# q in 512-byte packets, a state product on column tiles, a second issuing queue and a new order of the first loads in a fused retention and channel-mix kernel

## Chip, cores, metric

The kernel runs on one core of one Trainium2 chip. The metric is device time in microseconds (us) of one execution; lower is better. Some executions fall into a slower state of the chip, about 1.7% longer. Only fast executions are compared, and ratios are of executions on the same chip in the same rounds.

## The reference

Two layers follow each other. The first is a linear attention with a decay per head (4 batches, 8 heads, 768 tokens, 64 elements a head); the second is a channel mix with weights of 512x1024, 1024x512 and 512x512.

```python
for t in range(S):                       # retention, per batch b and head h
    state = gamma[h] * state + outer(k[t], v[t])
    y[t] = (q[t] @ state) / sqrt(D)
x = y.transpose(0, 2, 1, 3).reshape(B, S, H * D)
x_prev = shift x by one token
xk = mu_k * x + (1 - mu_k) * x_prev      # and xr with mu_r
k = maximum(xk @ w_k, 0)
out = sigmoid(xr @ w_r) * (k * k @ w_v)
```

## The kernel before

Tokens go in 24 chunks of 128 (six a batch). Each chunk is loaded as k, q, v with eight heads side by side, cast to 16 bits, and transposed on TensorE, so that the elements of two heads lie on 128 partitions. Then four products follow, named here by the letters used throughout: A (k with q, two heads at a time on two row tiles of the array), Y (v with the masked A, on two column tiles), I (the state of the last chunk with q, on the full array, since the state is kept block-diagonal for two heads) and S (the new state). The channel mix has Z (with w_k), R (with w_r) and V (with w_v). A list scheduler inside the kernel decides, from estimated durations, in which order each engine's instructions are emitted, and puts "filler" matmuls, whose results nobody reads, where it expects TensorE to be idle in the first 60 us. Constants at the top steer it.

```python
BLOCKS = {0: ((1,), (1,), (1, 1), (1, 1)), 3: ((1, 1), (1, 1), (1,), (1,))}
STORE = 5.0
FIRST = "k0 c2 q0 c16 c32 v0 k1 q1 v1 mu wk0 k2 q2 v2 wk1 wr k3 q3 v3 wv0 k4 q4 v4 wv1".split()
# ...
    def filler(b):
        nc.tensor.matmul(b.tile[:, 0:256], lhsT=warm[:, 0:P], rhs=warm, start=True, stop=True)
# ... every load: 128 tokens on partitions, 8 heads of 64 floats: 256 B runs
            src = s[b, :, c * C : (c + 1) * C, :].rearrange("h t d -> t h d")
            ... nc.sync.dma_start(out=t32.tile[:, n], in_=src)
# ... A: row tiles r = partitions 0:64 and 64:128
                nc.tensor.matmul(
                    pA.tile[:, hp, j], lhsT=t[r, 1, j, :], rhs=t[r, 0, j, :], ...)
# ... I: full array, four matmuls
                for j in range(NJ):
                    nc.tensor.matmul(
                        y()[:, j, :], lhsT=s_prev.tile[:, j], rhs=qkT.tile[:, 0, j, :],
                        start=(j == 0), stop=False, skip_group_check=True)
# ... Y: column tiles, eight matmuls into the same accumulator
            for j, hp, r in heads:
                nc.tensor.matmul(
                    y()[r, j, :], lhsT=v16.tile[:, 2 * j + hp, :], rhs=a2t.tile[:, hp, j, :], ...)
```

Of the kernel before, what the change touches and what calls it, by code (L numbers as in the profile page):

```python
# [21 lines left out]
BLOCKS = {0: ((1,), (1,), (1, 1), (1, 1)), 3: ((1, 1), (1, 1), (1,), (1,))}  # L22
BLOCKS_ELSE = ((2,), (2,), (2,))
STORE = 5.0
FIRST = "k0 c2 q0 c16 c32 v0 k1 q1 v1 mu wk0 k2 q2 v2 wk1 wr k3 q3 v3 wv0 k4 q4 v4 wv1".split()
BUFS = dict(t32=5, qks=3, v16=5, qkT=3, a2t=3, xT=2, dx=1, xk=2, xr=1, krel=3, k2=8, rsb=4,
            osb=5, w32=4)
COST = dict(qk=0, qkT=4000, relu=300, mask=0, dx=4000, s=500, v=0, w=800)
# [30 lines left out]
class Plan:  # L59
# [21 lines left out]
    def order(self):  # L81
        taken = {tag: [] for tag in self.bufs}
        free = {e: 0.0 for e in self.LAT}
        free["DMA"] = 1100.0
# [120 lines left out]
def kernel(  # L205
# [12 lines left out]
    nc = tc.nc  # L218
# [13 lines left out]

    gam = 1.0 - 2.0 ** (-5.0 - np.arange(H, dtype=np.float64))
    ar = np.arange(C, dtype=np.float64)
    h_pj = 2 * np.arange(NJ)[None, :] + (np.arange(P) // 64)[:, None]
# [10 lines left out]
    dec = [0.125 * gam[None, :] ** (ar + (par - 1) * C)[:, None] for par in range(2)]  # L246
# [3 lines left out]
    causal_np = (ar[None, :] >= ar[:, None]).astype(np.float64)  # L250
# [74 lines left out]

    def dma(dur, out_, in_):
        return Way("DMA", dur, lambda: nc.sync.dma_start(out=out_, in_=in_))  # L327
# [17 lines left out]
    nc.scalar.preload_act_table(AF.Sigmoid)  # L345
# [4 lines left out]
    k_c16 = add(first("c16"), dma(200, c16, c16d.ap()))  # L350
    d0 = add(first("mu"), dma(50, murow[0:4], moe_mu_k.rearrange("(co ci) -> co ci", ci=P)))
# [16 lines left out]
    def weight(dkey, key, w16, wd):  # L368
# [3 lines left out]
        def wide():  # L372
# [4 lines left out]
            dve(1230, lambda: nc.vector.tensor_copy(out=w16, in_=wide()), port=True),  # L377
# [5 lines left out]
    for i in range(2):  # L383
        fs = slice(i * dff // 2, (i + 1) * dff // 2)
        k_wk.append(weight(first(f"wk{i}"), -1.0, wk16[:, :, fs], wkd[:, :, fs]))
# [5 lines left out]
    heads = [(j, hp, slice(hp * 64, hp * 64 + 64)) for j in range(NJ) for hp in range(2)]  # L391

# [3 lines left out]
    def load(bt, b, c):  # L396
# [4 lines left out]
        for i, s in enumerate((k, q, v)):  # L401
            n = (1, 0, 2)[i]
            src = s[b, :, c * C : (c + 1) * C, :].rearrange("h t d -> t h d")
            bt.ld[c].append(add(
                first("kqv"[i] + str(g), g - LA[2] - 0.6 + 0.01 * i), Way("DMA", 1350, lambda n=n, src=src: nc.sync.dma_start(  # L405
                    out=t32.tile[:, n], in_=src)),
                after=[Order(x) for x in bt.ld[c][-1:]],
                takes=[] if i else [t32], uses=[t32] if i else []))

    def attention(bt, b, c):  # L410
# [5 lines left out]
        pT, pA, a2t, pY = Buf("px"), Buf("pA"), Buf("a2t"), Buf("px")  # L416
        e_qks = add(key, [
            dve(690, lambda: nc.vector.tensor_copy(out=qks.tile, in_=t32.tile[:, 0:2]), port=True),
            act(1010, lambda: nc.scalar.copy(out=qks.tile, in_=t32.tile[:, 0:2]),  # L419
# [12 lines left out]
        def do_T():  # L432
            o = pT.tile.bitcast(F16).rearrange("p (a j c) -> p a j c", a=2, j=NJ)
            for j in range(NJ):
                for i in range(2):
# [13 lines left out]

        def do_A():  # L450
            t = qkT.tile
            for j, hp, r in heads:
                nc.tensor.matmul(  # L453
                    pA.tile[:, hp, j], lhsT=t[r, 1, j, :], rhs=t[r, 0, j, :],
# [4 lines left out]
        def mask(i, takes, uses, after):  # L459
# [7 lines left out]
                out=a2t.tile[:, i], in_=a2t.tile[:, i], pattern=[[0, NJ], [1, C]],  # L467
# [7 lines left out]
        if c + 1 < NCH:  # L475
# [5 lines left out]
            def do_S():  # L481
                for j in range(NJ):
                    nc.tensor.matmul(  # L483
                        pS.tile[:, j], lhsT=qks.tile[:, 1, 2 * j : 2 * j + 2, :],
                        rhs=v16.tile[:, 2 * j : 2 * j + 2, :],
# [29 lines left out]
        if c > 0:  # L515
            def do_I():
                for j in range(NJ):
                    nc.tensor.matmul(  # L518
                        y()[:, j, :], lhsT=s_prev.tile[:, j], rhs=qkT.tile[:, 0, j, :],
                        start=(j == 0), stop=False, skip_group_check=True)  # L520

            e_I = add(key + 0.3, pe(220, do_I), after=[e_qkT, e_sprev], takes=[pY],
                      uses=[qkT, s_prev], mode="full")

        def do_Y():
            for j, hp, r in heads:
# [176 lines left out]
```

## Time and profile before

| | before |
|---|---|
| time, median of the runs beside the kernel after | 177.98 us (177.04 to 179.74) |
| span of the profiled execution | 176.0 us |
| TensorE busy | 170.0 us (97%) |
| VectorE busy | 142.6 us (81%) |
| first V, in effect | 38.8 us |
| end of the last V | 172.1 us |

"First V in effect" is the start of the fifth V matmul, the first that needs the second half of w_v, minus four matmuls of 0.2155 us. The end of the last V is the start of its last matmul plus 0.2155. The first V in effect is the mark at which the start, bound by transfers, hands over to the stretch bound by TensorE. The views that show these two regimes are in the prediction below. From the first V in effect to the end of the last is 133.3 us; the emitted matmuls and changes of mode make 132.2 of it.

### The profile page before, as it was taken

How to read it: one execution, taken by the hardware profiler on the slowest of the kernel's cores; microseconds unless marked ns; L12 is line 12 of the kernel's file. 1: busy time of each engine (PE TensorE's matmuls, PEld its weight loads, DVE VectorE, ACT ScalarE, POOL GpSimd, SP SyncE). 2: the span in 40 equal slices, each digit the busy share in tenths (PEclk: the TensorE clock that was granted, in tenths of full speed). 3: DMA queues.
4: the chain of work that ended last, by engine and by line, in shares of the span. 5: the costliest groups of instructions: out<-in, count | busy, mean ns of one | idle time of the engine just before them, and what ended most of it. 6: DMA issues, size and time to landing. Idle time of an engine off the chain costs nothing.

```text
span 176.0 us, 4319 instructions
## 1 busy us (share of the span) xinstructions
PE 170.0 (97%) x1777; PEld 116.5 (66%) x1777; DVE 142.6 (81%) x248; ACT 114.8 (65%) x161; POOL 45.9 (26%) x55
## 2 busy tenths in 40 slices
PE   7999999999999999999999999999999999899991
PEld 5587977866956766756758658648477567494850
DVE  0377797969879989999989899999998945897731
ACT  2432266554997876978965958969759575755550
POOL 3041010111433425237351263333214103400000
PEclk9999999999999999999999999999999999999999
DMA  4999999799989989899999967927330013010202
GB/s 105 231 300 268 378 199 308 178 298 192 234 171 249 253 202 264 208 240 233 228 260 227 261 117 187 255 46 186 112 119 4 0 63 119 2 62 24 96 29 94
DMA packets 81304, 30.79 MB, mean 175 GB/s; under 512 B 75514, under 2 KB 75650, under 8 KB 81284
## 3 DMA queue, kind: packets, MB, share of 16 engines
q1 hardware_dynamic: 81284, 30.51, 72.6%
q8 instruction: 14, 0.23, 0.6%
q14 instruction: 6, 0.05, 0.1%
HBM read 24.22 MB, written 6.29 MB: 173 GB/s over the span
## 4 chain that ended last, share of the span: by engine, by line
PE 72%; SPq 14%; DVE 5%; DMA 4%; ACT 2%; issue 1%; DVEq 0%; ACTq 0%
PE pm L639 24%; PE pm L603 21%; SPq L405 11%; PE pm L632 10%; PE px L436 5%; DMA t<-in_q_dram 4%; PE pA L453 3%; PE px L527 3%; PE px L518 2%; PE pS L483 2%; SPq L375 2%; SPq L327 2%; PE pm L277 1%; DVE xr L572 1%; PE pS L492 1%
## 5 line engine op out<-in xcount | busy, mean ns | idle before, releaser
L466 POOL TENSOR_SCALAR_AFFINE_SELECT a2t<-a2t 128x512 f16<-128x512 f16 x31 | 23.9, 783 | 89.7 <-ACT a2t L464 87.7
L603 PE MATMUL pm<-xk,wk 128*128 128x128 f16 (+1 forms) x576 | 47.0, 237 | 0.0
L639 PE MATMUL pm<-wv,k 128*128 128x512 f16 x192 | 44.9, 379 | 0.5 <-ACT k L622 0.5
L603 PEld LDWEIGHTS <-wk 128*128 128x128 f16 x576 | 40.1, 98 | 4.5 <-DVE wk L377 0.4
L446 ACT COPY qkT<-px 128x1024 f16<-128x1024 f16 x24 | 24.2, 1012 | 16.8 <-PE px L436 16.6
L639 PEld LDWEIGHTS <-k 128*128 128x128 f16 x192 | 18.0, 98 | 20.9 <-ACT k L622 0.7
L616 ACT ACTIVATE krel<-pm 128x512 f32<-128x512 f32 x34 | 20.3, 600 | 15.1 <-PE pm L603 14.8
L572 DVE SCALAR_TENSOR_TENSOR xk<-dx,mu,xT 128x256 f16<-128x256 f32 (+1 forms) x56 | 27.9, 537 | 0.1
L572 DVE SCALAR_TENSOR_TENSOR xr<-dx,mu,xT 128x256 f16<-128x256 f32 (+1 forms) x56 | 25.9, 498 | 1.0 <-PE pm L632 0.9
L622 ACT ACTIVATE k<-krel 128x1024 f16<-128x1024 f32 x24 | 25.4, 1060 | 0.3
L424 POOL TENSOR_TENSOR v<-t,c_sb 128x512 f16<-128x512 f32 x17 | 20.7, 1219 | 17.1 <-DMA t<-in_v_dram 13.0
L277 PE MATMUL pm<-warm 128*128 128x256 f16 x164 | 23.6, 290 | 1.1 <-DVE xT L536 1.1
L650 DVE SCALAR_TENSOR_TENSOR osb<-pm,rsb 128x512 f32<-128x512 f32 x24 | 16.4, 684 | 10.2 <-PE pm L639 5.0
L632 PE MATMUL pm<-wr,xr 128*128 128x512 f16 x96 | 24.2, 380 | 0.0
L464 ACT CAST a2t<-pA 128x512 f16<-128x512 f32 x31 | 17.4, 588 | 9.4 <-PE pA L453 7.2
L277 PEld LDWEIGHTS <-warm 128*128 128x128 f16 x164 | 15.8, 103 | 5.5 <-DVE xT L536 1.1
L419 ACT CAST qks<-t 128x1024 f16<-128x1024 f32 x16 | 16.7, 1052 | 2.4 <-DMA t<-in_q_dram 2.4
L542 DVE TENSOR_TENSOR xT<-px,Gy 128x512 f32<-128x512 f32 x24 | 16.3, 681 | 0.8 <-PE px L527 0.8
L645 ACT ACTIVATE rsb<-pm 128x512 f32<-128x512 f32 x24 | 14.0, 602 | 4.0 <-PE pm L632 3.9
L462 DVE TENSOR_TENSOR a2t<-pA,c_sb 128x512 f16<-128x512 f32 x17 | 11.6, 688 | 5.1 <-ACT a2t L464 4.7
L563 DVE TENSOR_TENSOR dx<-xT 128x1024 f32<-128x1024 f32 (+1 forms) x14 | 15.3, 1090 | 0.3
L436 PE MATMUL px<-c_sb,qks 128*128 128x128 f16 x192 | 14.5, 219 | 0.1
(34 smaller groups left out, 131.2 us busy)
## 6 DMA issues: line engine op xcount, KB each, us to landing
t<-in_k_dram SPq DMA_DIRECT2D x24, 256.0 KB, 4.6
t<-in_q_dram SPq DMA_DIRECT2D x24, 256.0 KB, 5.2
t<-in_v_dram SPq DMA_DIRECT2D x24, 256.0 KB, 5.3
out_dram<-osb SPq DMA_DIRECT2D x24, 256.0 KB, 3.8
w<-in_moe_w_k_dram SPq DMA_DIRECT2D x2, 1024.0 KB, 6.5
w<-in_moe_w_v_dram SPq DMA_DIRECT2D x2, 1024.0 KB, 7.4
w<-in_moe_w_r_dram SPq DMA_DIRECT2D x1, 1024.0 KB, 9.4
c_sb<-c SPq DMA_DIRECT2D x1, 64.0 KB, 3.7
```

Source lines behind the costliest of these rows:

```text
L277: nc.tensor.matmul(b.tile[:, 0:256], lhsT=warm[:, 0:P], rhs=warm, start=True, stop=True)
L405: first("kqv"[i] + str(g), g - LA[2] - 0.6 + 0.01 * i), Way("DMA", 1350, lambda n=n, src=src: nc.sync.dma_start(out=t32.tile[:, n], in_=src)),
L424: return lambda: engine.tensor_tensor(out=v16.tile, in0=t32.tile[:, 2], in1=Gv[par].unsqueeze(2).broadcast_to([P, H, D]), op=ALU.mult)
L436: nc.tensor.transpose(o[:, i, j, :], qks.tile[:, i, 2 * j : 2 * j + 2, :], ident)
L446: act(1010, lambda: nc.scalar.copy(out=qkT_out(), in_=pT.tile.bitcast(F16))),
L466: f = add(key + 0.2, pool(700, lambda: nc.gpsimd.affine_select(out=a2t.tile[:, i], in_=a2t.tile[:, i], pattern=[[0, NJ], [1, C]], compare_ ...
L572: (200 + TM) / 0.96, lambda w=w, o=o, co=co: nc.vector.scalar_tensor_tensor(out=cut(o)[:, co], in0=cut(dx)[:, co], scalar=mu[:, w * NCO + ...
L603: nc.tensor.matmul(o[:, n], lhsT=wk16[:, co, fo * P : fo * P + P], rhs=cut(xk)[:, co, t0 : t0 + TM], start=(co == 0), stop=(co == NCO - 1))
L616: act(600, lambda pZ=pZ, o=r_out: nc.scalar.activation(out=o(), in_=pZ.tile, func=AF.Relu, scale=KSC)),
L622: e_sq.append(add(kz + 0.05, act(1060, lambda krel=krel, k2=k2: nc.scalar.activation(out=k2.tile, in_=krel.tile, func=AF.Square)), after=e ...
L632: nc.tensor.matmul(pR.tile, lhsT=cut(xr)[:, co, t0 + ts.start : t0 + ts.stop], rhs=wr16[:, co, :], start=(co == 0), stop=(co == NCO - 1))
L639: nc.tensor.matmul(pV.tile, lhsT=o[:, n, ts], rhs=wv16[:, fo, :], start=(fo == 0), stop=(fo == NFO - 1))
```

## The change

The intent has four parts. q is loaded two tokens at a time, so that a packet has 512 B instead of 256; each q load becomes two, one for even and one for odd heads, each into every second row. This permutes q's tokens within a chunk (columns with a stride of two) and the heads that share a column block. I then is run head by head on column tiles, eight matmuls of half the width. The constants of the scheduler were searched anew; chunk 4 now follows all weights. And the first q load and the constants are issued from ScalarE's queue, ahead of the load of ScalarE's function table.

```diff
-FIRST = "k0 c2 q0 c16 c32 v0 k1 q1 v1 mu wk0 k2 q2 v2 wk1 wr k3 q3 v3 wv0 k4 q4 v4 wv1".split()
+FIRST = "k0 q0 c2 c16 c32 mu v0 k1 q1 v1 k2 q2 v2 wk0 wk1 k3 q3 v3 wr wv0 wv1".split()
+BY_ACT = ("q0", "c2", "c16", "c32", "mu")
 # BLOCKS, STORE, BUFS, COST: other values (cut)
+            def q_load(src=src, name=name):
+                for i in range(2):
+                    queue(name).dma_start(
+                        out=t32.tile[i::2, 0].rearrange("p (h s) d -> p h (s d)", s=2),
+                        in_=src.rearrange("(h i) (p s) d -> i p h (s d)", i=2, s=2)[i])
 # cast of q and k: rearranged heads (cut); A:
-                    pA.tile[:, hp, j], lhsT=t[r, 1, j, :], rhs=t[r, 0, j, :],
+                    pA.tile[:, hp, j], lhsT=t[r, 1, j, :], rhs=q_cols(j, r),   # [..., i::2]
 # I:
-                for j in range(NJ):
+                for j, hp, i, yj in cols2:
                     nc.tensor.matmul(
-                        y()[:, j, :], lhsT=s_prev.tile[:, j], rhs=qkT.tile[:, 0, j, :],
+                        y()[i * 64 : i * 64 + 64, yj, :], lhsT=s_prev.tile[:, j, hp],
+                        rhs=q_cols(j, slice(0, P)), ...)
-            e_I = add(key + 0.3, pe(220, do_I), ..., mode="full")
+            e_I = add(key + 0.3, pe(240, do_I), ..., mode="col")
 # the square of relu may also go to GpSimd; x is written with a stride of two (cut)
```

More of the change, by code (lines that the diff above doesn't have):

```diff
@@ L21 @@
 LA = (2.0, 0.4, 3.5)
-BLOCKS = {0: ((1,), (1,), (1, 1), (1, 1)), 3: ((1, 1), (1, 1), (1,), (1,))}
+BLOCKS = {0: ((1,), (1,), (1,), (1,), (1, 1)), 3: ((2,), (2,), (1, 1))}
 BLOCKS_ELSE = ((2,), (2,), (2,))
-STORE = 5.0
-FIRST = "k0 c2 q0 c16 c32 v0 k1 q1 v1 mu wk0 k2 q2 v2 wk1 wr k3 q3 v3 wv0 k4 q4 v4 wv1".split()
-BUFS = dict(t32=5, qks=3, v16=5, qkT=3, a2t=3, xT=2, dx=1, xk=2, xr=1, krel=3, k2=8, rsb=4,
+STORE = 4.0
+FIRST = "k0 q0 c2 c16 c32 mu v0 k1 q1 v1 k2 q2 v2 wk0 wk1 k3 q3 v3 wr wv0 wv1".split()
+BY_ACT = ("q0", "c2", "c16", "c32", "mu")
+BUFS = dict(t32=5, qks=3, v16=5, qkT=2, a2t=2, xT=2, dx=1, xk=3, xr=1, krel=2, k2=6, rsb=4,
             osb=5, w32=4)
-COST = dict(qk=0, qkT=4000, relu=300, mask=0, dx=4000, s=500, v=0, w=800)
+COST = dict(qk=0, qkT=1200, relu=300, mask=0, dx=4000, s=500, v=100, w=2000, wd=100, sq=200)
 class Buf:
@@ L83, in order @@
         free = {e: 0.0 for e in self.LAT}
-        free["DMA"] = 1100.0
+        free["DMA"], free["ACT"] = 1100.0, 4800.0
         left = {e: [] for e in self.LAT}
@@ L229, with head @@
     INV_KSC2 = 1.0 / (KSC * KSC)
+    def head(j, hp):
+        return 4 * (j // 2) + 2 * hp + j % 2
     gam = 1.0 - 2.0 ** (-5.0 - np.arange(H, dtype=np.float64))
     ar = np.arange(C, dtype=np.float64)
-    h_pj = 2 * np.arange(NJ)[None, :] + (np.arange(P) // 64)[:, None]
+    h_pj = np.array([[head(j, p // 64) for j in range(NJ)] for p in range(P)])
     own = (np.arange(P)[:, None] // 64 == np.arange(2)[None, :]).astype(np.float64)
@@ L244 @@
     c32_np = np.concatenate(cols, axis=1).astype(np.float32)
-    dec = [0.125 * gam[None, :] ** (ar + (par - 1) * C)[:, None] for par in range(2)]
+    tq = 2 * (np.arange(C) % 64) + np.arange(C) // 64
+    dec = [0.125 * gam[None, :] ** (tq + (par - 1) * C)[:, None] for par in range(2)]
     c2_np = np.concatenate(
@@ L249 @@
         axis=1).astype(np.float32)
-    causal_np = (ar[None, :] >= ar[:, None]).astype(np.float64)
+    causal_np = (tq[None, :] >= ar[:, None]).astype(np.float64)
     c16_np = np.concatenate([np.eye(P), causal_np], axis=1).astype(np.float16)
@@ L324, in pe, with queue @@
         return Way("PE", dur, emit)
+    def queue(name):
+        return nc.scalar if name in BY_ACT else nc.sync
     def dma(dur, out_, in_):
-        return Way("DMA", dur, lambda: nc.sync.dma_start(out=out_, in_=in_))
+        return Way("DMA", dur, lambda: nc.scalar.dma_start(out=out_, in_=in_))
     class Order:
@@ L344 @@
     nc.vector.memset(warm, 0.0)
-    nc.scalar.preload_act_table(AF.Sigmoid)
+    add(-97.0, act(0, lambda: nc.scalar.preload_act_table(AF.Sigmoid)))
     wkd = moe_w_k.rearrange("(co ci) f -> ci co f", ci=P)
@@ L376, in weight @@
         return add(key, [
-            dve(1230, lambda: nc.vector.tensor_copy(out=w16, in_=wide()), port=True),
+            dve(1230, lambda: nc.vector.tensor_copy(out=w16, in_=wide()), port=True, cost=COST["wd"]),
             act(1900, lambda: nc.scalar.copy(out=w16, in_=wide())),
@@ L384 @@
         fs = slice(i * dff // 2, (i + 1) * dff // 2)
-        k_wk.append(weight(first(f"wk{i}"), -1.0, wk16[:, :, fs], wkd[:, :, fs]))
+        k_wk.append(weight(first(f"wk{i}"), -1.0, wk16[:, :, fs], wkd[..., fs]))
     k_wr = weight(first("wr"), -0.9, wr16, wrd)
@@ L391 @@
     heads = [(j, hp, slice(hp * 64, hp * 64 + 64)) for j in range(NJ) for hp in range(2)]
+    cols2 = [(2 * a + i, hp, i, 2 * a + hp) for a in range(2) for hp in range(2) for i in range(2)]
     class Batch:
@@ L401, in load, with kv_load @@
         for i, s in enumerate((k, q, v)):
-            n = (1, 0, 2)[i]
-            src = s[b, :, c * C : (c + 1) * C, :].rearrange("h t d -> t h d")
+            src = s[b, :, c * C : (c + 1) * C, :]
+            name = "kqv"[i] + str(g)
+            def q_load(src=src, name=name):
[3 more added lines that the diff above has]
+                        in_=src.rearrange("(h i) (p s) d -> i p h (s d)", i=2, s=2)[i])
+            def kv_load(n=(1, 0, 2)[i], src=src):
+                nc.sync.dma_start(out=t32.tile[:, n], in_=src.rearrange("h t d -> t h d"))
             bt.ld[c].append(add(
-                first("kqv"[i] + str(g), g - LA[2] - 0.6 + 0.01 * i), Way("DMA", 1350, lambda n=n, src=src: nc.sync.dma_start(
-                    out=t32.tile[:, n], in_=src)),
+                first(name, g - LA[2] - 0.6 + 0.01 * i),
+                Way("DMA", (1350, 890, 1350)[i], (kv_load, q_load, kv_load)[i]),
                 after=[Order(x) for x in bt.ld[c][-1:]],
@@ L416, in attention, with cast_args @@
         pT, pA, a2t, pY = Buf("px"), Buf("pA"), Buf("a2t"), Buf("px")
+        def cast_args():
+            return dict(
+                out=qks.tile.rearrange("p n (a i h) d -> p (n a) i h d", a=2, i=2),
+                in_=t32.tile[:, 0:2].rearrange("p n (a h i) d -> p (n a) i h d", a=2, i=2))
         e_qks = add(key, [
-            dve(690, lambda: nc.vector.tensor_copy(out=qks.tile, in_=t32.tile[:, 0:2]), port=True),
-            act(1010, lambda: nc.scalar.copy(out=qks.tile, in_=t32.tile[:, 0:2]),
+            dve(690, lambda: nc.vector.tensor_copy(**cast_args()), port=True),
+            act(1010, lambda: nc.scalar.copy(**cast_args()),
                 cost=COST["qk"])],
@@ L448, in attention, with q_cols @@
             after=[e_T], takes=[qkT], uses=[pT])
+        def q_cols(j, r):
+            a, i = j // 2, j % 2
+            return qkT.tile[r, 0, 2 * a : 2 * a + 2, i::2]
         def do_A():
@@ L466, in mask @@
             f = add(key + 0.2, pool(700, lambda: nc.gpsimd.affine_select(
-                out=a2t.tile[:, i], in_=a2t.tile[:, i], pattern=[[0, NJ], [1, C]],
+                out=a2t.tile[:, i], in_=a2t.tile[:, i], pattern=[[0, NJ], [1, 2], [2, 64]],
                 compare_op=ALU.is_ge, fill=fill0, base=0, channel_multiplier=-1)),
@@ L484, in do_S @@
                         pS.tile[:, j], lhsT=qks.tile[:, 1, 2 * j : 2 * j + 2, :],
-                        rhs=v16.tile[:, 2 * j : 2 * j + 2, :],
+                        rhs=v16.tile[:, head(j, 0) : head(j, 0) + 3 : 2, :],
                         start=(j == 0 and par == 0), stop=(j == NJ - 1), skip_group_check=True)
@@ L516, in do_I @@
             def do_I():
-                for j in range(NJ):
+                for j, hp, i, yj in cols2:
                     nc.tensor.matmul(
-                        y()[:, j, :], lhsT=s_prev.tile[:, j], rhs=qkT.tile[:, 0, j, :],
-                        start=(j == 0), stop=False, skip_group_check=True)
-            e_I = add(key + 0.3, pe(220, do_I), after=[e_qkT, e_sprev], takes=[pY],
-                      uses=[qkT, s_prev], mode="full")
+                        y()[i * 64 : i * 64 + 64, yj, :], lhsT=s_prev.tile[:, j, hp],
+                        rhs=q_cols(j, slice(0, P)), start=(yj == 0), stop=False,
+                        skip_group_check=True)
+            e_I = add(key + 0.3, pe(240, do_I), after=[e_qkT, e_sprev], takes=[pY],
+                      uses=[qkT, s_prev], mode="col")
         def do_Y():
-            for j, hp, r in heads:
+            for j, hp, i, yj in cols2:
                 nc.tensor.matmul(
-                    y()[r, j, :], lhsT=v16.tile[:, 2 * j + hp, :], rhs=a2t.tile[:, hp, j, :],
-                    start=(j == 0 and c == 0), stop=(j == NJ - 1), skip_group_check=True)
-        e_Y = add(key + 0.3, pe(225, do_Y), after=[e_m0, e_m1, e_I],
+                    y()[i * 64 : i * 64 + 64, yj, :], lhsT=v16.tile[:, head(j, hp), :],
+                    rhs=a2t.tile[:, hp, j, :], start=(yj == 0 and c == 0), stop=(yj == NJ - 1),
+                    skip_group_check=True)
+        e_Y = add(key + 0.3, pe(240, do_Y), after=[e_m0, e_m1, e_I],
                   takes=[pY] if c == 0 else [], uses=[v16, a2t] + ([pY] if c else []), mode="col")
@@ L539, in x_out, with y_in @@
         def x_out():
-            return bt.x.tile[:, :, 1 + c * C : 1 + (c + 1) * C]
+            return bt.x.tile[:, :, 1 + c * C : 1 + (c + 1) * C].rearrange(
+                "p j (m i) -> p j i m", i=2)
+        def y_in(t):
+            return t.rearrange("p j (i m) -> p j i m", i=2)
         bt.e_x.append(add(key + 0.3, dve(690, lambda: nc.vector.tensor_tensor(
-            out=x_out(), in0=y(), in1=Gy[:, par], op=ALU.mult)),
+            out=x_out(), in0=y_in(y()), in1=y_in(Gy[:, par]), op=ALU.mult)),
             after=[e_Y, z, k_gy[par]], uses=[bt.x, pY]))
@@ L621, in moe_block @@
             if i % 2:
-                e_sq.append(add(kz + 0.05, act(1060, lambda krel=krel, k2=k2: nc.scalar.activation(
-                    out=k2.tile, in_=krel.tile, func=AF.Square)), after=e_r, takes=[k2],
-                    uses=[krel]))
+                e_sq.append(add(kz + 0.05, [
+                    act(1060, lambda krel=krel, k2=k2: nc.scalar.activation(
+                        out=k2.tile, in_=krel.tile, func=AF.Square)),
+                    pool(1900, lambda krel=krel, k2=k2: nc.gpsimd.tensor_tensor(
+                        out=k2.tile, in0=krel.tile, in1=krel.tile, op=ALU.mult), cost=COST["sq"])],
+                    after=e_r, takes=[k2], uses=[krel]))
         k2s = sorted({id(x[0]): x[0] for x in where.values()}.values(), key=id)
```

## The prediction

> **What bounds the kernel now.** I read the page first, then a table by stretches (busy time of each engine, then of the filler matmuls alone), then the chain of waits, then the timeline where the chain turns from a wait on a transfer to TensorE.
>
> ```profile
> PE   7999999999999999999999999999999999899991
> DVE  0377797969879989999989899999998945897731
> DMA  4999999799989989899999967927330013010202
> GB/s 105 231 300 268 378 199 308 178 298 192 234 171 249 253 202 264 208 240 233 228 260 227 261 117 187 255 46 186 112 119 4 0 63 119 2 62 24 96 29 94
> DMA packets 81304, 30.79 MB, mean 175 GB/s; under 512 B 75514, under 2 KB 75650, under 8 KB 81284
> ```
>
> TensorE looks full from the second slice, and so do the DMA engines until about 104 us. Nearly all packets are under 512 B: they are the 256 B rows (64 floats of a head) of q, k and v. A slice is 4.4 us. In the first 44 us the slices with little but such loads move 178 to 199 GB/s, the best slice, with weight loads (2 KB rows), 378.
>
> TensorE's fullness in the start is made of fillers. In the next two fences the columns are the stretch, its length, busy time and count of each engine, the clock, the DMA share and GB/s; the first has TensorE, weight loads, VectorE, ScalarE and GpSimd, the second TensorE and weight loads of the filler line alone.
>
> ```profile
> 0.00:34.00 34.00, 32.45 (x344) 24.84 (x344) 21.98 (x41) 14.95 (x20) 5.72 (x12) 1.00 0.98 245
> 77.00:104.00 27.00, 27.00 (x261) 17.30 (x256) 25.53 (x41) 22.24 (x32) 12.36 (x14) 1.00 1.09 237
> 104.00:140.00 36.00, 36.00 (x355) 23.78 (x354) 34.51 (x57) 27.50 (x39) 11.26 (x13) 1.00 0.45 111
> ```
>
> ```profile
> 0.00:34.00 34.00, 20.92 (x146) 14.14 (x146) 1.00 0.98 245
> 34.00:45.00 11.00, 2.69 (x21) 1.63 (x18) 1.00 1.02 248
> 45.00:172.00 127.00, 0.00 (x0) 0.00 (x0) 1.00 0.66 153
> ```
>
> So there are two regimes: a start bound by transfers, which ends where the last weight arrives, and a long stretch bound by TensorE, with VectorE 95% busy beside it (25.53 of 27, 34.51 of 36). The chain (start, length, what) and the timeline show the border:
>
> ```profile
> 26.31 7.12 DMA t<-in_q_dram
> 33.53 0.70 DVE qks L418
> 34.27 0.62 PE px L436 x8
> ...
> 37.40 0.33 PE pA L453 x8
> 37.73 1.09 PE pm L277 x9
> 38.82 3.56 PE pm L639 x16
> 42.39 0.45 PE px L436 x8
> ...
> 172.35 0.69 DVE osb L650
> ```
>
> ```profile
> 38.36 1.23 DVE L377 CAST wv<-w 128x2048 f16<-128x2048 f32 x1 [1.49 <-DMA w<-in_moe_w_v_dram]
> ```
>
> The second half of w_v lands at 38.3 us and is cast; the first product with w_v (L639, "V") begins at 38.8. From there to 172.3 is 133.5 us. How much of it is real work? Take issue times from the chain: V and the w_r product 0.2155 us a matmul, the w_k product 0.056 (128 columns) or 0.1105 (256), transposes 0.0556, the row- and column-tiled A and Y 0.028 each (pairs run together), state products 0.055. A group of eight A takes 0.33 instead of 0.224 and the V after it 1.83 instead of 1.73: each change between full, row-tiled and column-tiled array costs about 0.108 us. Over the emitted order, work after the first V is 124.7 us, and 69 changes cost 7.5: 132.2 of 133.5. TensorE hardly stalls there. The chain's detour through ScalarE and VectorE at 68 to 77 us is no stall either: the matmuls in it sum to the same 8.3 us.
>
> **What the Trainium skill says.** (1) "DMA: Bandwidth & Descriptors", Specifications, gives 512 B as the smallest transfer for line rate. The trace agrees in direction: about 185 GB/s with 256 B rows against up to 378 with 2 KB rows; it has no 512 B rows. (2) The same page, "Issuing engines are not separate DMA queues": a second issuing engine saves only issue time. The trace of before has one queue, so doesn't show it. (3) "TensorE: Matmul & The Clock Gate", Part 3, says that column tiles run concurrently. Agreed: eight Y matmuls fit in 0.34 us with one change of mode. (4) "SBUF — State Buffer", Door 1, on 16-byte lines: strides up to eight 16-bit elements are free. The q operand of A and I becomes a stride of two; no run yet shows whether it is free.
>
> **The change, part by part.**
>
> *q in 512 B packets.* A 256 B load runs at about 185 GB/s, 1.4 us for 262 KB; a 1 MB weight at 378, 2.75 us. Check: when q of chunk 3 lands (25.95 us), 11 loads and 3 weights have passed, 15.4 + 8.25 + 2.5 us of beginning = 26.15; when q of chunk 4 lands (33.4), 14 loads and 4 weights give 33.1. Per engine that is 21.9 ns for 256 B and 86 ns for 2 KB, so 12.7 ns fixed and 28 B/ns; 512 B cost 31 ns, a q load 0.99 us (estimate). It saves 0.4 us a load, 1.6 us before the first V. After the start the DMA engines hold nothing up, so the other 20 save nothing.
>
> *Order of loads.* The new order sends four chunks and all five weights before chunk 4; the old one had chunk 4 and most of its v ahead of the last weight. Needed for the first V: 8 k and v loads x 1.4 + 4 q x 1.0 + 5 weights x 2.75 + 0.3 of constants = 29.3 us. In the old kernel the same sum for w_v (37.3) came 1 us early against 38.3, so I add 0 to 1.
>
> *Two queues.* k0 and q0 no longer wait for each other's issue (0.4 to 0.5 us each); the first slice, 4 tenths busy, fills a little. I take the beginning as 2.0 instead of 2.5 us. The last weight thus lands at 31.3 to 32.3 us. V's first four matmuls need only the first half, so V starts in effect at the end of the cast minus 0.9: 31.8 + 0.2 + 1.2 - 0.9 = 32.3, that is 6.5 us earlier than 38.8.
>
> *What it gives back on TensorE.* The work is the same, 137.8 us in both. But before the first V the old order has 13.0 us of it, the new one 10.9: 2.2 more come after. The state product on column tiles keeps its time (8 x 0.028 instead of 4 x 0.055) but changes mode: 102 changes instead of 87 in all, after the first V 8.6 us instead of 7.5. Fifteen fillers stand after the first V, 1.6 us; none did. So 126.9 + 8.6 + 1.6 = 137.1 us follow, against 132.2.
>
> *Stalls and tail.* Before had 1.3 us of stalls. The new order ends in "w_k product, w_r product (0.86), V": that V needs an eviction of 0.60 and a square of 1.06 with some latency, about 2.0 after the w_k product, so it stalls about 1.1. The old end had another V there. I take 2.0. After the last V both need 3.7 us (the result, its store).
>
> *VectorE.* Counted in the order: casts of q and k 11 for 8 (0.79 each), relu 10 for 14 (0.68), v 5 for 7, s 17 for 18: -2.5 us. The rearranged cast and the xT write of stride two I take at their old times. GpSimd and ScalarE have room.
>
> Sum: 32.3 + 137.1 + 2.0 + 3.7 = 175.1 us of span against 176.0. The timed median was 2.1 above the span: 177.2.
>
> **The rivals.** (a) *The fillers and stalls are soft*: the 15 fillers stand where TensorE would wait anyway, and the others are saved. Then 1.6 and up to 2.0 fall out: span 171.5, time 173.6. For it: the mix of constants looks tuned as a whole. Against: TensorE had no slack after its first V. (b) *Strided operands are slow*: if the stride of two halves the moving rate, A and I cost 0.22 more each, 44 times: +9.7 us, time about 187. Only a skill page speaks against it. (c) *VectorE takes over*: if the rearranged cast loses its double speed (0.5 us x 11) or the xT write slows, VectorE, already 95% busy, would bind: +2 to +6, time 179 to 183. (d) *512 B in every second row is no faster*: +1.6 us, time 178.8.
>
> **Range and chances.** The working gives 177.2; (a) seems likelier than (b), (c) and (d) together, as the change reads like a whole that was tuned, so I put the time at 175.8 us, 8 in 10 within 172.8 and 179.2. Over 2% faster means under 174.5, which needs most of (a): 0.33. Slower by over 2% needs (b) or the worst of (c): 0.07. Within 2%: 0.60.
>
> **What would show it.** Right: the last w_v cast begins near 32 us, the first V near 32 to 33 (old 38.8); packets under 512 B drop by some 24,600; fillers 138; A and I keep 0.33 us a group; V at the end waits about 1 us. Wrong: a first V later than 34 us (DMA step), A or I groups over 0.4 us (b), qks casts on VectorE over 0.9 us or xT over 0.8 (c), TensorE idle for more than 3 us after the first V, or a sum of useful matmul time after the first V far from 137.

## The result, and the profile after

The kernel after took 180.3 us (median of 4 runs, 179.90 to 180.65) against 177.98 for the kernel before beside it. A ratio here and below is taken over the fast runs of both kernels in the same rounds, so it is not quite the ratio of the medians: 1.0147, 95% interval 1.0098 to 1.0197. That is slower, but by less than 2%. It lies 1.1 us above the upper end of the predicted range. The span went from 176.0 to 177.8 us, both at full granted clock.

First the page of the kernel after, the slices and the packets:

```profile
PE   7799989899999999999999999999999999999971
DVE  0358985988999988989999987988889797686211
DMA  6999999989999966997998998402030030110211
GB/s 142 195 259 379 225 303 392 248 197 221 248 260 279 254 161 178 268 244 190 278 217 246 247 213 231 125 21 102 4 118 0 0 122 2 59 62 29 89 63 59
DMA packets 69400, 30.79 MB, mean 173 GB/s; under 512 B 51322, under 2 KB 63746, under 8 KB 69380
```

Packets under 512 B fell by 24,192, nearly the 24,576 of q. The transfers end earlier than before. But TensorE, which was at nine tenths or more in every slice from the second to the 34th, now has a seven in the second and eights in slices 6 and 8.

Next the table by stretches (columns as in the prediction; a DMA share over 1.00 means that the times of packets overlap in the records), then the same of the filler line alone:

```profile
0.00:34.00 34.00, 30.45 (x337) 22.31 (x338) 21.10 (x39) 16.36 (x24) 7.24 (x14) 1.00 0.98 271
21.00:23.00 2.00, 0.91 (x12) 0.51 (x10) 2.00 (x4) 0.60 (x1) 0.36 (x1) 1.00 0.40 94
77.00:104.00 27.00, 27.00 (x277) 17.71 (x272) 26.07 (x45) 20.00 (x30) 9.01 (x11) 1.00 1.03 239
```

```profile
0.00:34.00 34.00, 18.23 (x123) 11.67 (x123) 1.00 0.98 271
34.00:45.00 11.00, 0.27 (x1) 0.10 (x1) 1.00 0.89 207
45.00:172.00 127.00, 2.31 (x14) 1.24 (x14) 1.00 0.59 150
```

In the first 34 us 271 GB/s flow instead of 245. From 21 to 23 us, however, the DMA engines are only 0.40 busy. And 15 fillers stand behind the first V, where there were none.

The timeline where the start hands over, TensorE and the casts of w_v:

```profile
31.47 2.03 PE L286 MATMUL pm<-warm 128*128 128x256 f16 x16
33.34 1.02 PE L688 MATMUL pm<-wv,k 128*128 128x512 f16 x4
33.60 1.23 DVE L390 CAST wv<-w 128x2048 f16<-128x2048 f32 x1 [0.33 <-DMA w<-in_moe_w_v_dram]
34.88 1.02 PE L688 MATMUL pm<-wv,k 128*128 128x512 f16 x4 [0.51 <-DVE wv L390]
```

The first V begins at 33.34 behind 16 fillers; its second four wait 0.51 us for the cast of the weight that landed at 33.57. In effect the first V is at 34.88 - 0.86 = 34.0, not 38.8: 4.8 us earlier. The chain of waits shows the end:

```profile
168.60 1.80 PE pm L649 x32
170.43 0.61 ACT krel L662
171.05 1.06 ACT k L669
...
172.16 1.91 PE pm L688 x8
```

The last V waits for an eviction and a square, as predicted. It ends at 173.9, 1.8 us later than before. So the 4.8 us are gone and 1.8 more: from the first V in effect to the end of the last are now 139.9 us instead of 133.3. The emitted order and the trace give the 6.6 us that were added:

| after the first V, us | before | after | more |
|---|---|---|---|
| useful matmuls | 124.7 | 126.9 | 2.2 |
| fillers | 0 | 1.6 | 1.6 |
| changes of mode (0.108 us each) | 7.5 | 8.6 | 1.1 |
| rest: stalls | 1.1 | 2.8 | 1.7 |
| measured | 133.3 | 139.9 | 6.6 |

The rest is the measured stretch minus the three counted terms. As idle time of TensorE behind the mark the timeline shows 0.9 us ahead of the last V (1.1 by issue times) and 0.45 in three small pieces; the other 1.3 is spread over the stretch and not seen as idle time. The wait at the fifth V lies ahead of the mark.

What the new operands cost is in the groups by form (busy us and mean ns of one after the bar):

```profile
L493 PE MATMUL pA<-qkT 64*128 64x128 f16 x192 | 9.7, 219 | 0.0
L452 DVE CAST qks<-t 128x1024 f16<-128x1024 f32 x11 | 8.5, 772 | 6.1 <-DMA t<-in_q_dram 6.1
L558 PE MATMUL px<-qkT,s 128*64 128x128 f16 x160 | 7.7, 223 | 0.0
L588 DVE TENSOR_TENSOR xT<-px,Gy 128x512 f32<-128x512 f32 x24 | 16.4, 687 | 2.8 <-PE px L568 2.4
```

The rearranged cast takes 772 ns (788 before), the strided xT write 687 (681). A with the stride of two has 219 ns a record (218 before), but the ends of matmul records are modelled, so the test is the time from the start of a group of eight to what follows: 333 to 338 ns, against 330 before. None got slower by more than 0.01 us.

### The profile page after: what moved, and what is told of

Read it like the earlier page. It is cut to its first block, busy times and chain, and to the rows that moved or that the text cites. A ratio compares the mean times of both kernels' runs of the same rounds, so it can differ in the third digit from the quotient of the medians.

```text
span 177.8 us, 4333 instructions
## 1 busy us (share of the span) xinstructions
PE 168.6 (95%) x1767; PEld 112.3 (63%) x1767; DVE 139.5 (78%) x244; ACT 115.3 (65%) x164; POOL 44.6 (25%) x57
## 4 chain that ended last, share of the span: by engine, by line
PE 71%; DVE 11%; SPq 9%; DMA 5%; issue 1%; ACT 1%; ACTq 1%; DVEq 0%
PE pm L649 20%; PE pm L688 20%; PE pm L681 10%; SPq L424 6%; PE px L471 5%; PE pA L493 3%; PE px L568 3%; SPq L429 3%; PE pm L286 3%; PE px L558 3%; DMA c_sb<-c 3%; DVE xr L618 2%; DMA t<-in_q_dram 2%; DVE xk L618 2%; PE pS L523 2%; DVE xT L588 2%
## 5 line engine op out<-in xcount | busy, mean ns | idle before, releaser
L649 PE MATMUL pm<-xk,wk 128*128 128x128 f16 (+1 forms) x512 | 46.0, 246 | 1.1 <-DVE wk L390 1.1
L649 PEld LDWEIGHTS <-wk 128*128 128x128 f16 x512 | 39.1, 98 | 6.4 <-DVE wk L390 1.5
L506 POOL TENSOR_SCALAR_AFFINE_SELECT a2t<-a2t 128x512 f16<-128x512 f16 x31 | 22.5, 737 | 80.4 <-ACT a2t L504 68.8
L662 ACT ACTIVATE krel<-pm 128x512 f32<-128x512 f32 x38 | 22.4, 596 | 14.3 <-PE pm L649 13.9
L618 DVE SCALAR_TENSOR_TENSOR xr<-dx,mu,xT 128x256 f16<-128x256 f32 (+1 forms) x56 | 26.6, 514 | 0.9 <-PE pm L681 0.9
L618 DVE SCALAR_TENSOR_TENSOR xk<-dx,mu,xT 128x256 f16<-128x256 f32 (+1 forms) x56 | 25.9, 501 | 0.1
L286 PE MATMUL pm<-warm 128*128 128x256 f16 x138 | 20.8, 286 | 1.1 <-DVE xT L578 1.1
L453 ACT CAST qks<-t 128x1024 f16<-128x1024 f32 x13 | 13.6, 1050 | 3.9 <-DMA t<-in_q_dram 3.9
L286 PEld LDWEIGHTS <-warm 128*128 128x128 f16 x138 | 13.0, 102 | 4.2 <-DVE xT L578 1.1
L471 PEld LDWEIGHTS <-qks 128*128 128x128 f16 x192 | 12.4, 98 | 3.6 <-issue 0.8
```

The lines of the kernel that those rows point to most:

```text
L471: nc.tensor.transpose(o[:, i, j, :], qks.tile[:, i, 2 * j : 2 * j + 2, :], ident)
L506: f = add(key + 0.2, pool(700, lambda: nc.gpsimd.affine_select(out=a2t.tile[:, i], in_=a2t.tile[:, i], pattern=[[0, NJ], [1, 2], [2, 64]], ...
L618: (200 + TM) / 0.96, lambda w=w, o=o, co=co: nc.vector.scalar_tensor_tensor(out=cut(o)[:, co], in0=cut(dx)[:, co], scalar=mu[:, w * NCO + ...
L649: nc.tensor.matmul(o[:, n], lhsT=wk16[:, co, fo * P : fo * P + P], rhs=cut(xk)[:, co, t0 : t0 + TM], start=(co == 0), stop=(co == NCO - 1))
L662: act(600, lambda pZ=pZ, o=r_out: nc.scalar.activation(out=o(), in_=pZ.tile, func=AF.Relu, scale=KSC)),
```

## The experiments

Each ran five rounds beside the kernel before. All traces are single executions. "Work after V" is the stretch from the first V in effect to the end of the last.

| run | ratio to before (95% interval) | span | first V in effect | work after V: measured / counted |
|---|---|---|---|---|
| before | 1 | 176.0 | 38.8 | 133.3 / 132.2 |
| after | 1.0147 (1.0098 to 1.0197) | 177.8 | 34.0 | 139.9 / 137.1 |
| e1 layout alone | 1.0185 (1.0137 to 1.0233) | 179.1 | 39.1 | 136.1 / 134.7 |
| e2 schedule alone | 1.0192 (1.0155 to 1.0230) | 179.3 | 34.9 | 140.5 / 137.3 |
| e3 one queue | 1.0153 (1.0111 to 1.0195) | 178.3 | 34.1 | 140.2 / 137.1 |
| e4 no late fillers | 1.0101 (1.0036 to 1.0166) | 177.5 | 34.7 | 138.9 / 135.5 |
| e5 I by Y | 1.0064 (0.9997 to 1.0130) | slow | | |
| e6 layout, I by Y | 1.0019 (0.9975 to 1.0064) | 175.7 | 38.1 | 133.8 / 132.7 |
| e7 e6, fillers cut | 0.9964 (0.9913 to 1.0014) | slow | | |
| e8 before, fillers cut | 1.0013 (0.9957 to 1.0069) | 175.3 | 37.9 | 133.5 / 132.2 |
| e9 I by Y, no late fillers | 1.0019 (0.9981 to 1.0057) | 176.6 | 35.5 | 137.2 / 134.5 |
| e10 weights by ScalarE | 1.0324 (1.0271 to 1.0376) | 182.4 | 39.4 | 139.1 / 137.1 |
| e11 before, I by Y | 1.0012 (0.9972 to 1.0051) | slow | | |
| e12 w_r early | 1.0185 (1.0116 to 1.0253) | 180.1 | 36.5 | 139.7 / 137.1 |
| e13 all | 1.0089 (1.0051 to 1.0127) | 178.8 | 36.5 | 138.3 / 134.5 |

"Slow": the profiled execution fell into the slow state, so its trace is not read; its ratio is from fast runs. "Counted" is useful matmuls, fillers and changes of mode from the emitted order. All results were correct.

**e1 and e2: layout alone, schedule alone.** My theory of the result was that the new layout and the new schedule each cost something that the earlier loads had to pay for. e1 is the kernel after with the constants and the scheduler's numbers of before, so that the work of every engine has the old order; e2 is the kernel before with the new constants.

```diff
 # e1 (after):
-FIRST = "k0 q0 c2 c16 c32 mu v0 k1 ..."          +FIRST = "k0 c2 q0 c16 c32 v0 k1 ..."
-            Way("DMA", (1350, 890, 1350)[i], ...   +            Way("DMA", 1350, ...
-            e_I = add(..., pe(240, do_I), ..., mode="col")
+            e_I = add(..., pe(220, do_I), ..., mode="full")
 # e2 (before): the new FIRST, BLOCKS, STORE, BUFS, COST, start of ScalarE, and the square on GpSimd too
```

> The old kernel with the new q load and the column-tiled state product alone, one queue, the old order of work on every engine. Changes of array mode rise from 87 to 115, of those after the first V from 69 to about 92, 2.4 us at 0.108 each. From the measured packet times (256 B 19.9 ns, 512 B 31.9 ns) a q load takes 1.02 instead of 1.27 us, so five of them let the last weight land 1.2 us earlier, at about 37.1 us, with the first V at 37.5. Theory 'mode changes and transfers trade': -1.2 + 2.4, so 1.2 us over before, about 179.2. Theory 'the split q load spoils the transfers': first V no earlier than 38.8, 180.4 or more. Theory 'the layout is free': 176.8.

> The new constants (order of loads, blocks, buffers, costs) on the old q load and layout, one queue. After the first V 126.2 us of matmuls, 8.0 of mode changes, 29 fillers (3.1). Theory 'the schedule is what loses': the last weight lands about 1 us later than in the changed kernel (four q loads at 0.25 more), first V near 34.5, and VectorE is behind between 45 and 57 us; 181 to 182.5. Theory 'the layout is what loses': under 178.

Each alone is slower than before by 1.9%; the two together are no slower than either. In e1 the first V is where it was (39.1), though loads were shorter: in the old order fillers precede V, and they do not vanish when data come early. Its work after V grew by 2.8 us; 28 more changes of mode, 2.4 us of them after V, account for most. By its time, 181.1 us, and its first V e1 falls where I had put 'the split q load spoils the transfers'; but the weight landed at 37.0, as I had expected of the shorter loads (37.1), so it was not the transfers that held V. What I had left out is the fillers. e2 came out as its first theory said. The first V came 3.9 us earlier, and the work after it grew by 7.2 us: 1.5 of useful work, 3.1 of fillers (29), 0.5 of changes and 2.1 of stalls. That the two do not add fits the count: the schedule of the kernel after knows of the new mode (102 changes instead of e1's 115) and has 15 late fillers instead of 29.

**e3: one queue.**

```diff
-BY_ACT = ("q0", "c2", "c16", "c32", "mu")
+BY_ACT = ()
-        return Way("DMA", dur, lambda: nc.scalar.dma_start(out=out_, in_=in_))
+        return Way("DMA", dur, lambda: nc.sync.dma_start(out=out_, in_=in_))
```

> The changed kernel with all loads issued from SyncE, all else in the same order. Theory 'the second queue helps the beginning': the first V comes 0.5 us later, 180.8. Theory 'ScalarE's start (table load at 6.4 us, first copy at 9.4 instead of 8.1) costs': 179.5. Theory 'the issue that was held up at 12.6 to 17.7 us sets the last weight': no change, 180.3, with the same starved stretch at 20 to 24 us.

1.0153 against 1.0147: no difference in time that these runs could show. The last weight landed at 33.7 us instead of 33.6.

One thing does differ: TensorE's mean granted clock, which the record lists for each run. It is 0.995 or more in all 42 fast executions of the one-queue kernels (e1 to e3, e6 to e8, e11) and in all of the kernel before. With two queues (after, e4, e5, e9, e10, e12, e13) it is 0.991 or less in 30 of 44. In the traces of e9, e10, e12 and e13 the clock is at half for 3.4 to 6.8 us between 8 and 16 us; here is e9's, by slices of 4.4 us:

```profile
PEclk9969999999999999999999999999999999999999
```

The trace of the kernel after keeps the full clock, and its two runs at 0.99 are no slower than its other two, so this does not explain its loss. e3 is the only run that takes the second queue alone away: none of its six runs is at the lower clock, against two of four. Whether the queue brings it, and how, is not shown.

**e4: without the fillers behind the first V.** This tests rival (a), that they stand where TensorE would wait anyway.

```diff
+    fills = itertools.count()
     def filler(b):
-        nc.tensor.matmul(b.tile[:, 0:256], ...)
+        if next(fills) < 123:
+            nc.tensor.matmul(b.tile[:, 0:256], ...)
```

> The changed kernel without the 15 filler matmuls that stand after the first V; nothing else moves. If TensorE is what binds at 45 to 57 us: 1.6 us less, 178.7. If VectorE binds there, as its chain of 14 us from 42.8 to 57.2 says: under 0.4 us less, 180.0 to 180.3.

The ratio fell from 1.0147 to 1.0101 (the intervals overlap), about 0.8 us of time; in the traces the work after V fell by 1.0 us of the 1.6 that the fillers took. So the fillers are partly soft: 0.6 us of them was waiting that comes back as stalls. In the kernel after VectorE is busy for 24.5 of the 26 us from 34 to 60, and the chain of waits runs over it between 43 and 57 us.

**e5, e6, e11: I right ahead of Y.** If the changes of mode are what the layout costs, I must gain by standing beside Y, which uses the same column tiles. Before each Y the emission puts I's matmuls, where no buffer that they read is taken again meanwhile. This leaves the work as it is and cuts the changes from 102 to 86 in the kernel after (e5) and from 115 to 89 in e1 (e6).

```diff
+            if ok:                       # ok: no buffer that I reads is taken again before Y
+                emit_i, emit_y = t.emit, y.emit
+                t.emit = None
+                y.emit = lambda i=emit_i, z=emit_y: (i(), z())
 ...
+        if e_I is not None:
+            e_I.ahead_of = e_Y
```

> The changed kernel with the column-tiled state product moved right ahead of the Y matmuls, which are column-tiled too; nothing else moves. Changes of array mode fall from 102 to 86, those after the first V by 10, 1.0 us at 0.108 each. Theory 'mode changes cost what the sum says': ratio to before from about 1.015 to 1.009, 179.2. Rival 'the state product was better early, out of Y's way': no gain or a loss, 180.3 or more.

> e1_layout (new layout in the old order) with the same move: 115 changes of mode become 89, those after the first V fall by about 21, 2.2 us, with 0.2 us more work after it. Theory 'e1_layout lost its 3 us to mode changes': from 1.0185 to 1.007, 179.1 against 178 to 178.7 of before. Rival 'strided operands or the 64-column weight loads lost it': stays near 1.018.

The chain of waits of e1 has I (L558) alone between two groups of V (L685):

```profile
102.92 1.83 PE pm L685 x8
104.75 0.35 PE px L558 x8
105.10 1.83 PE pm L685 x8
```

And that of e6 has I (L583) and Y (L593) together:

```profile
100.46 0.35 PE px L583 x7
100.81 0.23 PE px L593 x8
101.04 3.56 PE pm L712 x16
```

Alone, I takes 0.35, and the V behind it 1.83 instead of 1.73: 0.45 us for what took 0.22 before. (Of I's eight matmuls in e6 the chain counts the first to the step before.) Beside Y, the pair takes 0.58 instead of Y's 0.34 alone, so I costs 0.24, about as before. e6 brought the ratio from 1.0185 to 1.0019, and the work after V fell by 2.3 us, where 2.0 were counted (2.2 fewer changes, 0.2 more useful work behind V). e5 gained less, 1.0147 to 1.0064, where 1.0 us was counted after V.

The control e11 makes the same move in the kernel before, where I uses the full array. There the changes stay at 88 instead of 87.

> A control to e6: the kernel before, whose state product uses the full array, with the same move of its matmuls to right ahead of Y's. That leaves the changes of mode at 88 instead of 87 (after the first V 7.6 us instead of 7.5), where in the new layout it took them from 115 to 89. If e6 gained by changes of mode, this is 1.000 (0.997 to 1.004). If the move gains something else (a later need of the state, better filled gaps), it gains here too: about 0.985 to 0.99.

1.0012, within the expectation of no gain. So it is not the later place of I that gained in e6, but the changes of mode. This settles the layout: with I beside Y it costs, together with the new q load, nothing that these runs resolve; in the place where the scheduler had put it, it costs 1.9% in the old order.

**e7 and e8: fewer fillers ahead of the first V.** In e6 the loads are early and TensorE does not notice. e7 leaves out the last 18 fillers ahead of V; e8 does so in the kernel before, as a control.

```diff
-        nc.tensor.matmul(b.tile[:, 0:256], ...)
+        if not 146 <= next(fills) < 164:
+            nc.tensor.matmul(b.tile[:, 0:256], ...)
```

> e6_layout_i_by_y without the last 18 fillers ahead of the first V. In e1_layout the last weight landed at 37.0 us, 1.3 us earlier than before, but the first V stayed at 39.1, behind nine fillers that run from 38.1. Theory 'fillers kept the faster loads from counting': the fifth V starts near 38.4 instead of 39.9 and the time falls by another 1.3 us, ratio 0.999 to 1.0. Rival 'something else holds V (masks, evictions)': no change against e6.

> Control: the kernel before without the same 18 fillers. There the fifth V starts at 39.64, 0.05 us after the cast of the last weight ends, so it waits for the weight: no change (ratio 0.998 to 1.001). If it gains 0.5 per cent or more, the fillers held the old kernel too, and the gain of e7 isn't one of the faster loads.

e7 is the only kernel below the kernel before, 0.9964, but its interval includes 1. e8 is 1.0013: there the weight lands at 37.5 us, and the fifth V starts at 38.8. The step from e6 to e7, half a per cent, is what the shorter q packets may bring once fillers make room; these runs do not resolve it.

**e9: I by Y and no late fillers in the kernel after.** It tells whether fillers and changes are separate terms or two sides of one bound on VectorE.

```diff
 # e5 and e4 together
-        nc.tensor.matmul(b.tile[:, 0:256], ...)
+        if not 123 <= next(fills) < 999:
+            nc.tensor.matmul(b.tile[:, 0:256], ...)
```

> The kernel after with the state product right ahead of Y (e5) and without the 15 fillers behind the first V (e4) together. e4 came to 1.0101 and e5 to 1.0064 of before, against 1.0153 and 1.0147 for the kernel with one queue and with two. If fillers and changes of mode are separate terms, their gains add: 1.0147 - 0.0046 - 0.0083 = about 1.002, span about 176.2. If VectorE is the bound in the stretch where both would gain (about 43 to 57 us), the gains overlap and it stays at about 1.006, no better than e5.

1.0019, as the sum of the two gains asked for. Eight of its eleven fast runs are at a clock of 0.990 or less, 178.99 us on average; the other three average 177.91, the kernel before 178.24. In the trace too the first V, at 35.5, was late by TensorE's own program, for the weight had landed at 33.8. Behind the first V the clock is full: work after V fell by 2.7 us against the kernel after; the counted fall is 1.6 + 1.0 = 2.6. So most of what made the kernel after slower than before was these two terms, and they add.

**e10, e12, e13: why did the last weight land late?** In the kernel after, w_r was issued late on SP. The timeline of SP's queue (start, length, the loads):

```profile
12.57 5.80 SPq L424 DMA_DIRECT2D t<-in_q_dram  x2
18.41 0.60 SPq L429 DMA_DIRECT2D t<-in_v_dram  x1
19.06 2.48 SPq L388 DMA_DIRECT2D w<-in_moe_w_r_dram  x1
21.58 1.38 SPq L388 DMA_DIRECT2D w<-in_moe_w_v_dram  x2
```

The two halves of chunk 3's q took 5.8 us to issue, w_r 2.5; an issue that nothing holds up takes 0.4 to 0.7. In the gap that follows, 21 to 23 us, the DMA engines were at 0.40. e10 issues w_r and w_v from ScalarE's queue; e12 issues w_r ahead of chunk 3 instead of behind it, every compute engine keeping its order; e13 is e12 with the edits of e9 and without 16 more fillers ahead of V.

```diff
 # e10
-BY_ACT = ("q0", "c2", "c16", "c32", "mu")
+BY_ACT = ("q0", "c2", "c16", "c32", "mu", "wr", "wv0", "wv1")
 # e12
     def emit(self):
+        named = {getattr(t, "name", ""): t for t in self.tasks}
+        self.tasks.remove(named["wr"])
+        self.tasks.insert(self.tasks.index(named["k3"]), named["wr"])
 # e13: e9, the same lines as e12, and
-        if not 123 <= next(fills) < 999:
+        if not 107 <= next(fills) < 999:
```

> The kernel after with the loads of w_r and w_v issued from the ScalarE queue. In the kernel after, the issue of w_r on SP took 2.5 us (19.06 to 21.54), behind the loads of chunk 3, and the DMA engines fell to 0.44 and 0.35 busy at 21 to 23 us. If that hold-up belongs to the SP queue and causes the late last weight, w_r starts by about 20 us, the gap goes, the last half of w_v lands 1.0 to 1.5 us earlier (at about 32.3) and the first V starts in effect at about 32.7: span about 176.6, ratio about 1.008. If the hold-up is not the cause (the transfers themselves bound it, or the hold-up comes back on the other queue), the last half of w_v still lands at 33.5 or later and the ratio stays at 1.013 to 1.016.

> The kernel after with one load moved: w_r is issued ahead of chunk 3's k instead of behind chunk 3's v; every compute engine keeps its order. In the kernel after, w_r's issue lasted from 19.06 to 21.54 and the DMA engines were at 0.44 and 0.35 in the microseconds from 21 to 23. If that gap is what made the last weight late, it goes here, and the second half of w_v lands 1.0 to 1.4 us sooner, at 32.2 to 32.6. If the transfers themselves are the limit (a gap opens elsewhere), it lands at 33.3 to 33.8 again. Chunk 3 lands about 2.7 us later, and TensorE reaches its transposes (24.61 in the kernel after) late by 1 to 2 us, so the time need not gain: ratio 1.010 to 1.025 by either theory; the landing is what is tested.

> As e12, with the state product ahead of Y, without the 15 fillers behind the first V and without the last 16 ahead of it (1.7 us). If the first V follows the load, it starts in effect 1 to 1.5 us earlier than in e9 (35.5), and the time is 0.3 to 0.8 per cent under e9's: ratio 0.994 to 0.999. If chunk 3's later arrival holds TensorE, the first V is at 35 or later and the ratio is 1.000 to 1.006.

e10 did not test what it was made for: ScalarE reaches its issue only between its own work, w_r at 25.1 us, and the last packet of the weights started at 37.9 us, 5 us later than in the kernel after. It says one thing: the first V came 5.3 us later than in the kernel after, and the span grew by 4.6. The first V does set the time nearly one for one.

In e12 the gap of 21 to 23 us is closed, and another has opened where the first half of w_v, now behind chunk 3, was held in issue for 3.7 us. The table by stretches of e12:

```profile
21.00:23.00 2.00, 2.00 (x29) 1.31 (x28) 2.00 (x5) 1.25 (x4) 0.41 (x1) 1.00 1.22 274
24.00:25.00 1.00, 1.00 (x14) 0.64 (x11) 1.00 (x4) 0.35 (x1) 0.54 (x1) 1.00 0.40 99
```

The last weight landed at 33.0 us (33.6 in the kernel after), between what the two theories asked for; in e13, with the same loads, at 31.7. So a gap goes with a held-up issue of a weight behind q, k and v loads, and moving one load moves the gap. What holds an issue stays open: for chunk 3's q and w_r it is no wait that the program states (the earlier loads on whose completion they wait had landed by 12.9 us), and no run here took the cause away by itself. Neither kernel is faster for the earlier landing. The traces of these three runs have the lowered TensorE clock described under e3 (mean 0.98 over the span), so a part of their later first V may be the clock's; by the timed runs e13, for all its cuts, is behind e9. In e13 the cast of the last weight stood behind other work on VectorE, and the fifth V waited 1.35 us for it though the weight had landed at 31.7.

## Why the prediction was wrong

It predicted 175.8 us (172.8 to 179.2); 180.3 came. Its working had given a span of 175.1 us, against 177.8 measured: 32.3 + 137.1 + 2.0 + 3.7 was in fact 34.0 + 137.1 + 2.8 + 3.9. The miss of 4.5 us is thus 1.7 for the first V, 1.0 for stalls and tail, 0.4 for the step from span to time, and 1.4 by which I had left the working.

- **The regimes: right.** The first V does mark the border, and the counted work after it, with fillers and 0.108 us a change, is 137.1 of the 139.9 us. e6, e9 and e11 confirm the price of a change: counted gains of 2.0, 2.6 and none; measured 2.3, 2.7, and none in time.
- **The first V: too early by 1.7 us, the largest term.** The step that failed is the landing of the last weight, put at 31.3 to 32.3; it was 33.6. First, a q load saves less than the 0.4 us given. The packet records of the trace have 256 B at 19.9 ns before (my 21.9 was from the landing times) and 512 B at 31.9 (my estimate 31): 1024 x 19.9 / 16 = 1.27 us and 512 x 31.9 / 16 = 1.02 us, a saving of 0.25. In the first 34 us alone they took 20.3 before and 36.3 after, a saving of 0.14. With four q loads that is 0.6 to 1.0 us less than I gave. Second, the sum of transfers took the DMA engines as never idle; they lost 2 x 0.60 = 1.2 us at 21 to 23. These pieces overlap with errors of the other sign and are not a closed sum; why the landing was late stays open in part, as what holds an issue does. The landing also varies: with one order of loads it was 33.6, 33.7, 34.2 and 33.8 (after, e3, e4, e9; 31.8 in e5, a slow execution), with that of e12 and e13 33.0 and 31.7. Third, the working never added up TensorE's own program ahead of V: with its 123 fillers it came to the first V only at 33.3, so a weight at 31.3 would have met a TensorE still busy with fillers.
- **Two queues: right that it matters little.** I gave it 0.5 us; e3 shows nothing in time. That a clock could hang on it was not in the working.
- **Stalls and tail: too small by 1.0 us together.** By issue times the wait ahead of the last V was 1.1 us, as predicted; what lies beside it was put at 0.9 and came to 1.7, and most of that was not located. The tail was no miss: the working let the last V end 0.2 us later than the mark used here, by which the tail was 3.9 us before as well.
- **The step from span to time** was 2.5 us instead of 2.1, since the profiled execution was the fastest of the four; its own step was 2.1 (179.9 - 177.8). That my 2.1 fits it is luck: I took it from a median beside the kernel before, whose own profiled execution had 1.9 (177.85 - 176.0). In every run with the old q load the step is 1.7 to 1.9 us, in every run with the new one 2.0 to 2.3. So some 0.3 us of the new load's cost lies outside the span; its cause is not known.
- **Rival (a), to which I moved the number by 1.4 us: wrong.** The working said 177.2; I went to 175.8 since the change "reads like a whole that was tuned". e4 shows the late fillers to be soft by 0.6 us of 1.6 in a trace, and the other stalls did not fall out but grew. Left at the working, the number would have missed by 3.1 us instead of 4.5, and a range as wide around it, 174.2 to 180.6, would just have held the result.
- **Rivals (b) and (c): refuted.** A and I groups take 0.33 to 0.35 us, under the 0.4 that I named; the cast and the xT write did not slow. VectorE did bind in part, from 43 to 57 us, but by its order and not by slower operands.
- **Rival (d): half true.** 512 B packets are faster per byte, 64 against 80 ns per KB (31.9 x 2, 19.9 x 4; 73 against 81 in the first 34 us); at twice the rate it would have been 40.

What I had not weighed is that the layout could be good and its place bad. I counted the 1.1 us of changes of mode correctly, and did not ask whether they were needed: the skill has the rule. "TensorEngine Tiling (Array Packing)", Key Properties, says that changing the tiling mode, not just the tile, drains TensorE. The trace agrees: 0.108 us a change, and e6 gets back 1.7% by making fewer.

So where did the gain of the earlier start go? 4.8 us came in ahead of the first V. Of these, 2.2 were useful work only moved behind it, 1.6 fillers, 1.1 changes of mode, 1.7 stalls. With fillers and changes taken out (e9) the kernel is level with before, and no version here is faster by a margin that the runs resolve.

## What to carry to other kernels

Data that arrive earlier are worth only the idle time that they replace: count what moves behind the mark, and count the engine's own program ahead of it, fillers included. When an operation is moved to another mode of the array, put it beside one that uses the same mode already; the price of a change is paid by the neighbour as well. And when a working has been added up with care, a feeling that the change was tuned is no reason to leave it.

## What the Trainium skill lacked or had wrong

- "TensorEngine Tiling (Array Packing)", Key Properties: it says that a change of mode drains TensorE, without a size. Here it is about 0.108 us, and a lone group of eight half-width matmuls between full-width ones costs 0.45 us instead of 0.24 beside its like.
- "DMA: Bandwidth & Descriptors", Specifications: it gives 512 B as the smallest transfer for line rate. Here a packet of 256 B took 19.9 ns, of 512 B 31.9 ns and of 2 KB 90 to 98 ns, so 512 B is still well short of the rate of 2 KB.
- The same page, "Issuing engines are not separate DMA queues": it says that issue time is usually small beside the DMA. Here issues on one queue were held up to 6.3 us behind weights, and the DMA engines fell to 0.40 of their time for 2 us; no page that I found says what limits it.
- "SBUF — State Buffer", Door 1, had it right for the moving operand of a matmul: with the stride of two a group of eight A takes 333 to 338 ns against 330.
